# Where the attention stops stand inside the feed-forward slots: five per group, or four that cross the group borders

## The chip, the cores and the metric

One core of a Trainium2 chip runs the whole kernel. The metric is device time in microseconds (us), the median of several executions. PE is the matrix engine, ACT the scalar engine, DVE the vector engine, POOL the general engine (it issues the loads and scales v), and SP the engine that issues the output stores and the transposing DMAs.

## The reference

Retention with a decay per head, then a feed-forward block with a "snake" activation:

```
state = gamma[h]*state + k_t (outer) v_t ;  y_t = (1/sqrt(D)) * q_t @ state      # B=4, H=8, S=768, D=64
x = y laid out as [3072, 512]
h = x @ w_in                      # 512 -> 2048
g = h + sin(alpha*h)^2 / (alpha + 1e-9)
out = g @ w_out                   # 2048 -> 512, float32
```

## The kernel before

**Chunks and groups.** The recurrence is computed in chunks of 128 tokens: 6 chunks for each of 4 batches, 24 in all. They are worked on in the order `P`: P[0..3] are the first chunks of the four batches, then come chunks 1 to 5 of batch 0 (P[4..8]), of batch 1 (P[9..13]), of batch 2 (P[14..18]) and of batch 3 (P[19..23]). Consecutive chunks form groups 0 to 6 of `sizes = [4, 2, 4, 4, 4, 4, 2]` chunks: group 2 is P[6..9], group 3 P[10..13], group 4 P[14..17], group 5 P[18..21], group 6 P[22..23].

**What is done for a chunk j.**

- X(j), `turn`, L205: a transposing DMA on SP's queue writes `qkT` (6 buffers) from the raw `qkr`.
- A(j), `stage_A`: 8 matmuls `pa<-qkT` (L213) on 64-row tiles of PE give the scores, then one DVE multiply with the mask writes `aT` (L217, 2 buffers). `pa` has one buffer.
- M(j), `stage_M`: the mix. 8 matmuls `py<-qkT,s_bd` (L247) with the carried state, 8 matmuls `py<-aT,vr` (L251), and, unless j is the last chunk of its batch, 8 matmuls `ps<-vr,qkr` (L227, `stage_S`) that add to the state; all three are on 128x64 tiles. A DVE multiply writes the chunk's columns of `xT` (L258), and two ACT copies write `s_bd` (L234). `py` has one buffer.
- SK(j): the state of a first chunk, the 8 matmuls of L227 and the two ACT copies, by themselves. It is called ahead of the mix of chunk 1 of a batch.

**The feed-forward of a group.** `phase(g, outs, att, nf)` goes through slots. With `nf=1` there are 16 of them. A slot issues 4 matmuls `ph<-xT,w_in` (L279) of 512 columns, a sine (L282) and a square (L287) on ACT, then whatever stands in `att` for this slot number (a *stop*), then the DVE instruction that writes `gT` (L294), and then a share of `outs`: the matmuls `po<-w_out,gT` (L304) of the group before. A group of 4 tiles gives 64 of these, 4 per slot; group 1, whose two tiles are put out in phase 2, gives 2 per slot. When the 16th matmul of a tile is issued, ACT copies it out (L316) and SP stores it (L317). `ph` and `po` share 4 PSUM buffers, taken in turn.

In phase g the stops hold the attention of group g+1, whose `xT` the first slot of phase g+1 reads. The order on every engine is the order in which the code issues (`manual_schedule`).

Of the kernel before, what the change touches and what calls it, by code (L numbers as in the profile page):

```python
# [15 lines left out]
def kernel(  # L16
# [18 lines left out]
    NCH = S // C  # L35
    NJ = B * NCH
# [4 lines left out]
    FF = d_ff // 128  # L41
# [7 lines left out]
    sizes = [4, 2, 4, 4, 4, 4, 2]  # L49
    assert sum(sizes) == NJ  # L50
    NG = len(sizes)
    groups = [order[sum(sizes[:g]):sum(sizes[:g + 1])] for g in range(NG)]
    place = {j: (g, i) for g, js in enumerate(groups) for i, j in enumerate(js)}
# [148 lines left out]
    def turn(j):  # L202

        st["qkT", j] = work.tile([128, 2 * NP, 128], BF16, name="qkT", tag="qkT", bufs=6)
        nc.sync.dma_start_transpose(out=st["qkT", j], in_=raw["qk", j].rearrange("p i h d -> p (i h d)"))  # L205

    def stage_A(j):
        qkT = st["qkT", j]
        pa = psum.tile([128, 2, NP, 128], F32, name="pa", tag="pa")
        for p in range(NP):  # L210
            for e in range(2):
                r = slice(64 * e, 64 * e + 64)
                nc.tensor.matmul(pa[:, e, p, :], qkT[r, NP + p, :], qkT[r, p, :],  # L213
                                 start=(p == 0), stop=True, skip_group_check=True)
        aT = work.tile([128, 2, NP, 128], BF16, name="aT", tag="aT", bufs=2)
        m = dec.rearrange("p e n t -> p (e n) t") if j % NCH == 0 else mask_bc
        nc.vector.tensor_mul(aT.rearrange("p e n t -> p (e n) t"), pa.rearrange("p e n t -> p (e n) t"), m)  # L217
        st["aT", j] = aT

    def stage_S(j):  # L220
        c = j % NCH
        if c == 0:
            st["ps"] = psum.tile([128, NP, D], F32, name="ps", tag="ps")
        ps = st["ps"]
        for p in range(NP):
            for e in range(2):
                nc.tensor.matmul(ps[64 * e:64 * e + 64, p, :], raw["k", j][:, 2 * p + e, :], raw["v", j][:, 2 * p + e, :],  # L227
                                 start=(c == 0 and p == 0), stop=True, skip_group_check=True)
        return ps

    def keep_S(j, ps):
        for e in range(2):
            r = slice(64 * e, 64 * e + 64)
            nc.scalar.copy(s_bd[(j % NCH + 1) % 2][r, :, r], ps[r, :, :])  # L234

    def stage_M(j):
        c = j % NCH
        g, i = place[j]
        if g not in xT:
            xT[g] = work.tile([128, KS, sizes[g] * C], BF16, name="xT", tag="xT", bufs=3)  # L240
        qkT, aT, vs = st["qkT", j], st["aT", j], raw["v", j]
        py = psum.tile([128, NP, 128], F32, name="py", tag="ty")
        if c > 0:
            for p in range(NP):
                for e in range(2):
                    r = slice(64 * e, 64 * e + 64)
                    nc.tensor.matmul(py[r, p, :], s_bd[c % 2][:, p, r], qkT[:, p, :],  # L247
                                     start=(p == 0), stop=True, skip_group_check=True)
        for p in range(NP):
            for e in range(2):  # L250
                nc.tensor.matmul(py[64 * e:64 * e + 64, p, :], vs[:, 2 * p + e, :], aT[:, e, p, :],  # L251
                                 start=(c == 0 and p == 0), stop=True, skip_group_check=True)
        x = xT[g][:, :, i * C:(i + 1) * C]
        if c == 0:
            nc.scalar.copy(x, py)
            return
        ps = stage_S(j) if c < NCH - 1 else None
        nc.vector.tensor_mul(x, py, qg[:, c])  # L258
        if ps is not None:
            keep_S(j, ps)  # L260
# [40 lines left out]
    def ff_out(g, ts, f):  # L301
        if (g, ts) not in po:
            po[g, ts] = psum.tile([128, d_model], F32, name="po", tag="mm", bufs=4)
        nc.tensor.matmul(po[g, ts], gT[g][:, f, ts * C:(ts + 1) * C], w_out[:, f, :],  # L304
                         start=(f == 0), stop=(f == FF - 1))
        if f == FF - 1:
            take(g, ts)
# [28 lines left out]
    def out_pieces(g, tss):  # L336
        return [lambda ts=ts, f=f: ff_out(g, ts, f) for ts in tss for f in range(FF)]
# [54 lines left out]
    def phase(g, outs, att, nf=1):  # L392

        no, done = len(outs), 0
        for n in range(FF // nf):
            now = Slot(g, n * nf, nf=nf).sq("A")
            for fn in att.get(n, ()):
                fn()
            now.add()
            while done < no * (n + 1) * nf // FF:  # L400
                outs[done]()
                done += 1

    def T(j):
        return lambda: stage_T(j)

    def X(j):
        return lambda: turn(j)

    def A(j):  # L410
        return lambda: stage_A(j)

    def M(j):
        return lambda: stage_M(j)

    def SK(j):
        return lambda: keep_S(j, stage_S(j))
# [3 lines left out]
    P = order  # L421
# [6 lines left out]
    def early(f, tag="mm"):  # L428
        return Slot(0, f, (0, n3), tag=tag)

    a = early(0)
# [6 lines left out]
    a = early(2)  # L438
# [8 lines left out]
    a = early(5)  # L447
# [17 lines left out]
    a = Slot(0, 0, (n3, n4), 4)  # L465
    F((1,), (3,))
    a.sq("A").add()
    a = Slot(0, 8)
    b = Slot(0, 4, (n3, n4), 4)
    a.sq("A").add()  # L470
    a = Slot(0, 9)
# [5 lines left out]
    a = Slot(0, 11)  # L477
# [7 lines left out]
    a = Slot(0, 13)  # L485
# [6 lines left out]
    a = Slot(0, 15)  # L492
# [28 lines left out]
    def fill(n):  # L521
        for _ in range(n):
# [11 lines left out]
    phase(1, outs,  # L534
          {0: [X(P[8])], 1: [A(P[6])], 2: [T(P[7]), X(P[9])], 3: [A(P[7]), M(P[6])], 4: [X(P[10])],
           5: [A(P[8]), M(P[7])], 6: [X(P[11]), A(P[9]), M(P[8]), SK(e1)], 7: [M(P[9])]}, 2)
    for g in range(2, NG):
        att = {}
        if g + 1 < NG:
            js = groups[g + 1]  # L540
            for i, j in enumerate(js):
                a = i * FF // len(js) + 1
                n = P.index(j) + 2
                if n < NJ:
                    att.setdefault(a + 1, []).append(X(P[n]))
                att.setdefault(a, []).append(A(j))
                if i > 0:
                    att[a].append(M(js[i - 1]))
                if j % NCH == 1:
                    att[a].append(SK(j - 1))  # L550
            att.setdefault(FF - 2, []).append(M(js[-1]))
        phase(g, out_pieces(g - 1, range(sizes[g - 1])), att, 1 if sizes[g] > 2 else 2)
    for fn in out_pieces(NG - 1, range(sizes[-1] - 1)):
        fn()
    last_tile(NG - 1, sizes[-1] - 1)
# [28 lines left out]
```

## Time and profile before

| what | value |
|---|---|
| time, median of 5 | 218.57 us (218.03 to 219.02) |
| the profiled execution: time, span | 218.03 us, 216.3 us |
| PE, ACT, DVE busy | 203.8, 162.5, 128.5 us |
| phase 2 (slot 0 to slot 0 of phase 3, start of L279) | 64.86 to 90.72 us |
| phase 3 | 90.72 to 123.21 us |
| phase 4 | 123.21 to 155.45 us |
| phase 5 | 155.45 to 185.31 us |
| PE clock granted | 1.000 |

The span is the time from the first to the last instruction of one profiled execution; its own time lies 1.7 us above its span. The matmul records overlap, since matmuls are pipelined; the distance from one start to the next is what a matmul costs PE. Some matmul records are missing, so a row with x3 may stand for four.

### The profile page before, as it was taken

The page shows a single profiled execution, that of the slowest core. Times are in us where ns is not written, and L with a number is a line of the kernel's source. Part 1 is how long each engine was busy: PE and PEld are TensorE (multiplying, and loading weights), DVE is VectorE, ACT ScalarE, POOL GpSimd, SP SyncE. Part 2 cuts the span into 40 slices and gives each one's busy share as a digit, 9 for nine tenths or more (in the row PEclk, how much of TensorE's full clock was granted, in tenths as well). Part 3 has the DMA queues.
Part 4 walks back from the last instruction along what each step waited for, and adds up shares of the span by engine and source line. Part 5 has one row for each costly group of instructions (what it writes and reads, how often), then busy time and mean ns, then how long its engine had stood idle before and what let it go on. Part 6 is the DMA issues. An engine that isn't in the chain of part 4 may idle for free.

```text
span 216.3 us, 4276 instructions
## 1 busy us (share of the span) xinstructions
PE 203.8 (94%) x1658; PEld 108.9 (50%) x1685; DVE 128.5 (59%) x213; ACT 162.5 (75%) x311; POOL 90.1 (42%) x105
## 2 busy tenths in 40 slices
PE   7898899999889999999999999999999999999994
PEld 3544554466654544445445445455444444555554
DVE  4786669866896767766466556466554455433311
ACT  7688796758879898788778778769768878666630
POOL 8976334998669696696978100000000000000000
PEclk9999999999999999999999999999999999999999
DMA  8999999999999999999999946147111101111112
GB/s 126 148 193 187 206 207 169 154 138 242 143 141 199 141 141 163 127 142 170 134 173 156 69 97 75 25 99 75 28 48 52 48 0 48 52 48 48 52 48 97
DMA packets 100853, 24.93 MB, mean 115 GB/s; under 512 B 93393, under 2 KB 97889, under 8 KB 100833
## 3 DMA queue, kind: packets, MB, share of 16 engines
q0 software_dynamic: 77024, 13.37, 86.3%
q1 hardware_dynamic: 23808, 11.28, 28.8%
q8 instruction: 13, 0.21, 0.4%
q14 instruction: 8, 0.06, 0.1%
HBM read 27.27 MB, written 6.29 MB: 155 GB/s over the span
## 4 chain that ended last, share of the span: by engine, by line
PE 71%; DMA 15%; POOL 4%; DVE 3%; issue 2%; ACT 2%; POOLq 0%; DVEq 0%
PE po L304 32%; PE ph L279 29%; DMA qkr<-in_k_dram 8%; DMA w_in<-in_moe_w_in_dram 4%; DMA qkT<-qkr 3%; PE py L247 3%; PE pa L213 2%; POOL qkr L83 2%; PE py L251 2%; PE poh L327 2%; POOL vr L83 1%; DVE aT L217 1%; PE ps L227 1%; ACT s L282 1%; POOL w_out L94 1%
## 5 line engine op out<-in xcount | busy, mean ns | idle before, releaser
L294 DVE SCALAR_TENSOR_TENSOR gT<-s,rec_alpha,ph 128x512 bf16<-128x512 f32 (+3 forms) x120 | 74.2, 638 | 69.9 <-ACT s L287 69.4
L279 PE MATMUL ph<-xT,w_in 128*128 128x512 bf16 (+3 forms) x478 | 97.9, 336 | 0.7 <-DVE gT L294 0.2
L282 ACT ACTIVATE s<-ph,alpha_sb 128x512 f32<-128x512 f32 (+3 forms) x120 | 69.5, 601 | 34.0 <-PE ph L279 33.9
L304 PE MATMUL po<-w_out,gT 128*128 128x512 bf16 x344 | 90.7, 379 | 3.8 <-issue 2.9
L279 PEld LDWEIGHTS <-w_in 128*128 128x128 bf16 x480 | 45.5, 98 | 42.1 <-issue 1.5
L287 ACT ACTIVATE s<-s 128x512 f32<-128x512 f32 (+1 forms) x94 | 58.4, 621 | 2.6
L304 PEld LDWEIGHTS <-gT 128*128 128x128 bf16 x368 | 33.7, 98 | 36.3 <-issue 0.6
L112 POOL TENSOR_TENSOR vr<-vr,kg 128x512 bf16<-128x512 bf16 x21 | 22.0, 1057 | 19.5 <-DMA vr<-in_v_dram 19.1
L217 DVE TENSOR_TENSOR aT<-pa,mask 128x1024 bf16<-128x1024 f32 x20 | 24.4, 1221 | 0.4 <-PE pa L213 0.4
L83 POOL DMA_DIRECT2D vr<-in_v_dram x24 | 21.8, 909 | 3.8 <-DMA w_in<-in_moe_w_in_dram 1.7
L83 POOL DMA_DIRECT2D qkr<-in_q_dram x23 | 21.3, 926 | 3.7 <-DMA w_out<-in_moe_w_out_dram 1.7
L83 POOL DMA_DIRECT2D qkr<-in_k_dram x23 | 20.6, 894 | 3.8 <-DMA w_out<-in_moe_w_out_dram 3.3
L234 ACT CAST s_bd<-ps 64x256 bf16<-64x256 f32 x40 | 14.4, 359 | 2.6 <-PE ps L227 2.3
L316 ACT COPY o_sb<-po 128x512 f32<-128x512 f32 x23 | 13.1, 575 | 4.0 <-PE po L304 3.9
L258 DVE TENSOR_TENSOR xT<-py,qg 128x512 bf16<-128x512 f32 x20 | 13.7, 684 | 2.3 <-PE py L251 2.1
L213 PE MATMUL pa<-qkT 64*128 64x128 bf16 x192 | 9.5, 219 | 1.5 <-DMA qkT<-qkr 0.9
L345 PE MATMUL spare<-warm 128*128 128x512 bf16 x27 | 9.5, 476 | 1.4 <-DVE warm L131 1.2
L213 PEld LDWEIGHTS <-qkT 64*128 64x128 bf16 x192 | 5.4, 94 | 10.6 <-issue 6.7
L251 PE MATMUL py<-aT,vr 128*64 128x128 bf16 x192 | 9.5, 220 | 0.4 <-DVE aT L217 0.4
L247 PE MATMUL py<-qkT,s_bd 128*64 128x128 bf16 x160 | 8.3, 225 | 0.2 <-DVE xT L258 0.2
L251 PEld LDWEIGHTS <-vr 128*64 128x64 bf16 x192 | 6.8, 110 | 1.3 <-issue 1.0
L247 PEld LDWEIGHTS <-s_bd 128*64 128x64 bf16 x160 | 5.2, 109 | 4.3 <-issue 1.7
(61 smaller groups left out, 75.3 us busy)
## 6 DMA issues: line engine op xcount, KB each, us to landing
out_dram<-o_sb SPq DMA_DIRECT2D x23, 256.0 KB, 2.3
vr<-in_v_dram POOLq DMA_DIRECT2D x24, 128.0 KB, 6.5
qkr<-in_q_dram POOLq DMA_DIRECT2D x23, 128.0 KB, 5.4
qkr<-in_k_dram POOLq DMA_DIRECT2D x23, 128.0 KB, 5.6
w_in<-in_moe_w_in_dram POOLq DMA_DIRECT2D x4, 512.0 KB, 10.7
w_out<-in_moe_w_out_dram POOLq DMA_DIRECT2D x4, 512.0 KB, 14.6
qkT<-qkr SPq DMA_TRANSPOSE x17, 6.4
q<-in_q_dram SPq DMA_DIRECT2D x1, 256.0 KB, 3.2
```

Source lines behind the costliest of these rows:

```text
L83: nc.gpsimd.dma_start(out=t, in_=chunk_of(src, j))
L112: eng.tensor_mul(raw["v", j], raw["v", j], kg[:, j % NCH, :, None].to_broadcast([128, H, D]))
L213: nc.tensor.matmul(pa[:, e, p, :], qkT[r, NP + p, :], qkT[r, p, :], start=(p == 0), stop=True, skip_group_check=True)
L217: nc.vector.tensor_mul(aT.rearrange("p e n t -> p (e n) t"), pa.rearrange("p e n t -> p (e n) t"), m)
L234: nc.scalar.copy(s_bd[(j % NCH + 1) % 2][r, :, r], ps[r, :, :])
L247: nc.tensor.matmul(py[r, p, :], s_bd[c % 2][:, p, r], qkT[:, p, :], start=(p == 0), stop=True, skip_group_check=True)
L251: nc.tensor.matmul(py[64 * e:64 * e + 64, p, :], vs[:, 2 * p + e, :], aT[:, e, p, :], start=(c == 0 and p == 0), stop=True, skip_group_che ...
L279: nc.tensor.matmul(self.ph[:, m, :], w_in[:, i, f * 128:(f + 1) * 128], xT[g][:, i, self.lo:self.hi], start=(m == 0 and i == 0), stop=(i = ...
L282: nc.scalar.activation(out=self.s[:, m, :], in_=self.ph[:, m, :], func=ACTF.Sin, scale=alpha_sb[:, f:f + 1])
L287: nc.scalar.activation(out=self.s, in_=self.s, func=ACTF.Square)
L294: nc.vector.scalar_tensor_tensor(gT[self.g][:, f, self.lo:self.hi], self.s[:, m, :], rec_alpha[:, f:f + 1], self.ph[:, m, :], op0=ALU.mult ...
L304: nc.tensor.matmul(po[g, ts], gT[g][:, f, ts * C:(ts + 1) * C], w_out[:, f, :], start=(f == 0), stop=(f == FF - 1))
```

## The change

Before, the stops of phase g for a group of four are at slots 1, 5, 9, 13 and 14: A of the first chunk alone, three times A of a chunk with M of the chunk ahead of it, and M of the last chunk alone. For the group of two in phase 5 they are at 1, 9 and 14. X stands one slot behind its A.

Afterwards one list of stops runs through phases 2 to 5. Each stop holds A(P[n]), M(P[n-1]), the SK where it is due, and X(P[n+2]), whatever group these chunks belong to. A(P[10]) is by itself in slot 1 of phase 2. The stops are then:

| phase | before | after |
|---|---|---|
| 2 | 1: A10; 5: A11 M10; 9: A12 M11; 13: A13 M12; 14: M13 | 1: A10; 5: A11 M10; 8: A12 M11; 11: A13 M12; 14: A14 M13 SK |
| 3 | 1: A14 SK; 5: A15 M14; 9: A16 M15; 13: A17 M16; 14: M17 | 2: A15 M14; 6: A16 M15; 10: A17 M16; 14: A18 M17 |
| 4 | 1: A18; 5: A19 M18 SK; 9: A20 M19; 13: A21 M20; 14: M21 | 2: A19 M18 SK; 6: A20 M19; 10: A21 M20; 14: A22 M21 |
| 5 | 1: A22; 9: A23 M22; 14: M23 | 6: A23 M22; 14: M23 |

(Numbers are positions in `P`.) On SP, the turns of P[16] to P[23] come one output store earlier than before; those of P[12] to P[15] keep their place among the stores. No instruction is added or removed.

```
+    where = {10: (2, 1)}
+    for g in range(2, NG - 1):
+        first = P.index(groups[g + 1][0])
+        if len(groups[g + 1]) == 2:
+            slots = (6, 14)
+        else:
+            slots = (5, 8, 11, 14) if g == 2 else (2, 6, 10, 14)
+        for i, n in enumerate(slots):
+            where[first + i + 1] = (g, n)
+    atts = {g: {} for g in range(2, NG)}
+    def at(place, fn):
+        atts[place[0]].setdefault(place[1], []).append(fn)
+    for n in range(10, NJ + 1):
+        if n < NJ:
+            at(where[n], A(P[n]))
+        if n > 10:
+            at(where[n], M(P[n - 1]))
+        if n < NJ and P[n] % NCH == 1:
+            at(where[n], SK(P[n] - 1))
+        if n + 2 < NJ:
+            at(where[n], X(P[n + 2]))
     for g in range(2, NG):
-        att = {}
-        if g + 1 < NG:
-            js = groups[g + 1]
-            for i, j in enumerate(js):
-                a = i * FF // len(js) + 1
-                n = P.index(j) + 2
-                if n < NJ:
-                    att.setdefault(a + 1, []).append(X(P[n]))
-                att.setdefault(a, []).append(A(j))
-                if i > 0:
-                    att[a].append(M(js[i - 1]))
-                if j % NCH == 1:
-                    att[a].append(SK(j - 1))
-            att.setdefault(FF - 2, []).append(M(js[-1]))
-        phase(g, out_pieces(g - 1, range(sizes[g - 1])), att, 1 if sizes[g] > 2 else 2)
+        phase(g, out_pieces(g - 1, range(sizes[g - 1])), atts[g], 1 if sizes[g] > 2 else 2)
```

## The prediction

> **What bounds the kernel now.** I read the page's engine shares first, then the PE timeline of phases 2 to 5, then DVE, ACT and SP around the places that change.
>
> ```profile
> PE 203.8 (94%) x1658; PEld 108.9 (50%) x1685; DVE 128.5 (59%) x213; ACT 162.5 (75%) x311; POOL 90.1 (42%) x105
> ```
>
> PE is busy nearly all the time, and from 65 us to the end its timeline shows matmuls end to end. So the question is what a stop costs PE, and where PE waits. The unit is the distance between starts: four 512-column matmuls take 0.865 us, a plain slot with 4 output matmuls 1.727 us (L279 starts at 102.89 and 108.07 are three slots apart), one with 2 output matmuls 1.297 us. The border between phases 2 and 3, and a full stop in phase 4:
>
> ```profile
> 78.43 1.02 PE L279 MATMUL ph<-xT,w_in 128*128 128x512 bf16 x4 [0.18 <-ACT o_sb L316]
> ...
> 87.15 1.03 PE L279 MATMUL ph<-xT,w_in 128*128 128x512 bf16 x4
> 88.41 0.41 PE L247 MATMUL py<-qkT,s_bd 128*64 128x128 bf16 x8 [0.23 <-DVE xT L258]
> 88.64 0.42 PE L251 MATMUL py<-aT,vr 128*64 128x128 bf16 x8
> ...
> 89.42 1.03 PE L279 MATMUL ph<-xT,w_in 128*128 128x512 bf16 x4
> ...
> 92.45 1.03 PE L279 MATMUL ph<-xT,w_in 128*128 128x512 bf16 x4
> 93.41 0.40 PE L213 MATMUL pa<-qkT 64*128 64x128 bf16 x8
> 93.73 0.32 PE L227 MATMUL ps<-vr,qkr 128*64 128x64 bf16 x8
> ...
> 94.86 1.03 PE L279 MATMUL ph<-xT,w_in 128*128 128x512 bf16 x4
> ...
> 132.28 1.03 PE L279 MATMUL ph<-xT,w_in 128*128 128x512 bf16 x4
> 133.24 0.40 PE L213 MATMUL pa<-qkT 64*128 64x128 bf16 x8
> 133.56 0.41 PE L247 MATMUL py<-qkT,s_bd 128*64 128x128 bf16 x8
> 133.81 0.39 PE L251 MATMUL py<-aT,vr 128*64 128x128 bf16 x8
> 134.03 0.29 PE L227 MATMUL ps<-vr,qkr 128*64 128x64 bf16 x8
> ...
> 135.13 1.03 PE L279 MATMUL ph<-xT,w_in 128*128 128x512 bf16 x4
> ```
>
> A stop's price is the distance between the L279 rows around it less one plain slot:
>
> - full (A, M with its state, or A, M and SK; 132.28 to 135.13): 2.85 - 1.73 = 1.12.
> - A alone (124.93 to 127.10, and 157.18 to 159.34): 0.44.
> - A with SK (92.45 to 94.86): 0.68.
> - M with state alone (118.95 to 121.48, and 151.20 to 153.72): 0.80.
> - M without state alone (181.19 to 183.59): 2.40 - 1.73 = 0.67. The same thing at the end of phase 2 costs 89.42 - 87.15 - 1.30 = 0.97: it waits 0.30 for `py`, which the DVE multiply of the chunk ahead, one slot earlier, has not yet read.
>
> The other wait is the first row: slot 9 of phase 2 needs the PSUM buffer of the tile put out at slot 7, while ACT's copy ran from 77.81. Slot 8's L279 started at 76.79 (its L304 at 77.65 less 0.865), so slot 9 was due at 78.08; it came 0.35 late. Check: phase 2 takes 25.86; 16 x 1.297 + 0.44 + 3 x 1.12 + 0.67 = 25.22, so 0.64 is lost, which is 0.35 + 0.30. The same sum for phases 3 to 5 leaves nothing over 0.1.
>
> **What the Trainium skill says.** "TensorEngine Tiling (Array Packing)", section Key Properties: changing the tiling mode drains the TensorE. The trace agrees: 0.96 from an L279 row to the L213 behind it, where four matmuls take 0.865, so 0.10 per change. By this, A alone has two changes, M alone two, A with SK three, a full stop three; joining A and M saves one, joining A with SK and M saves two. The prices agree: 0.44 + 0.80 - 1.12 = 0.12, and 0.68 + 0.67 - 1.12 = 0.23. "PSUM — Partial Sum Buffer", section Engine vs sequencer instructions: VectorE and ScalarE are strict FIFO, and matmuls start in program order. So a late DVE multiply delays everything behind it, and a PE wait stops all of PE; the 88.41 row shows the second.
>
> **The change, part by part.** No work is added; the matmul counts stay.
>
> 1. Joins. M13 with A14 and SK: 0.23 saved, and the 0.30 wait goes, since the multiply that M13 waited for is now three slots back, not one. M17 with A18: 0.12. M21 with A22: 0.80 + 0.43 - 1.12 = 0.11. Sum 0.76, all on PE's path.
> 2. Slots 9 and 13 of phase 2 become 8 and 11. The prices stay; but the stop in slot 8 puts 1.12 of PE work ahead of slot 9's L279, which moves to 76.79 + 1.30 + 1.12 = 79.21. ACT's copy ends at 78.38 (77.81 + 0.57), so it hides, and 0.35 goes. If that cover fails, at most these 0.35 come back.
> 3. ACT in phase 2: sine and square are one per 1.30 us (81.91, 83.20, 84.50, 85.80), just PE's slot. A stop adds 0.73 of ACT copies to 1.12 of PE, so three slots with a stop are 4.63 against 5.01; in the one interval with the tile copy (0.54 between starts) they are 5.17. ACT is then 0.16 late, less than the 0.39 left over in the next. I price it at nothing. DVE: 3 x 0.66 + 1.14 + 0.60 = 3.7 of 5.01. `ph` buffers come back three slots on: slot 11's L279, at about 81.8, needs slot 8's `gT`, which behind mask and `xT` ends at about 81.0. Covered by 0.8.
> 4. The border 2 to 3. In slot 14 DVE must now do the mask of A14 before the `xT` of M13, which the first matmul of phase 3 reads. Slot 13 shows the sequence:
>
> ```profile
> 85.88 0.75 DVE L294 SCALAR_TENSOR_TENSOR gT<-s,rec_alpha,ph 128x512 bf16<-128x512 f32 x1 [0.55 <-ACT s L287]
> 86.54 1.22 DVE L217 TENSOR_TENSOR aT<-pa,mask 128x1024 bf16<-128x1024 f32 x1
> 87.68 0.68 DVE L258 TENSOR_TENSOR xT<-py,qg 128x512 bf16<-128x512 f32 x1
> ```
>
> Its L279 started at 84.73, so `xT` ends 3.63 behind the slot's start; phase 3 begins 2 x 1.30 + 1.12 = 3.71 behind it. The margin is 0.08: I take nothing, and 0 to 0.3 for the range (half a DVE instruction). At borders 3 to 4 and 4 to 5 slots are 0.43 longer, and the margin is 0.9.
> 5. Transposes and SP. A12 comes at 77.8, its turn lands at 75.3 (67.92 + 7.4); A13 at 82.8 against 79.3 (72.85 + 6.4). The tightest is A14:
>
> ```profile
> 78.90 1.43 SPq L205 DMA_TRANSPOSE qkT<-qkr  x1
> 83.40 1.23 SPq L205 DMA_TRANSPOSE qkT<-qkr  x1
> ```
>
> The first is X14, 7.1 to landing, so 86.0; A14's matmuls come at about 87.8 (before: 93.41). X15 lands at 91.5; A15 comes at 94.9. X14 stays behind the same store. X16 and later pass one store, so X16 goes at about 88.5, when its k has landed, in place of 92.83; the store behind it is not due before 91.5, and its issue ties up nobody, as three `o_sb` buffers stand behind it. POOL's order is unchanged, and its v scalings are early: P13 by 76.8 for a mix at 88, the first chunk of batch 2 by 71.1 for SK at 88.6.
>
> Sum: -0.76 - 0.35 = **-1.1 us**. Against the profiled execution (218.03, span 216.3) this gives 216.9 and a span of 215.2. That execution was the fastest of the five shown; taken off the median 218.57 it gives **217.5**. The last phase and the tail only start earlier.
>
> **The rivals.**
>
> - *Joins alone.* The slot 9 wait stays in another place, or the border `xT` is late by 0.3 or more: 0.35 of the gain is left or lost, so about -0.4 to -0.75, or 217.8 to 218.2. For it: the 0.08 margin, and ACT in step with PE with no slack in phase 2. Against: both covers are read off rows of the same sequence. Chance 0.23.
> - *Nothing comes of it.* Denser stops make DVE late in phase 2 by what the joins save; 218.6. For it: the chain sine, square, `gT`, mask, `xT` is 3.63 long in slots of 1.30. Against: the 1.3 us slack of DVE per three slots. Chance 0.07.
> - *Slower.* A14 is pulled forward by 5.6 us, its transpose is not. PE stops for whatever the transpose is late. It lands 1.8 ahead; landings run from 3.1 to 8.8 us. Only from about 10.6 us after issue (3.5 later than X14 took) are both the 1.8 and the gain used up and 0.66 lost, giving 219.2 or more. No turn took that long, but POOL's loads of 128 KB share the DMA engines in this stretch, and the load ahead of it can be late too. Chance 0.07.
>
> **How the numbers follow.** My forecast, -1.3 to -0.9, has the remaining 0.63. A measurement of this kernel can tell some 0.3%, 0.66 us, from no change. Faster than that are the forecast and about half of *joins alone*: 0.75. Within it are the other half and *nothing*: 0.18. Slower: 0.07. The range runs from 217.0 (the forecast's end, with 0.3 for the spread of medians) to 218.4, which takes in *joins alone*.
>
> **What would show it.** In the profile after: phase 2's first L279 to phase 3's takes 25.67 (before 25.86); phase 3 takes 32.11 (32.49), phase 4 32.11 (32.24), phase 5 29.42 (29.86). Every full stop costs 1.12. No wait for `o_sb` at slot 9 and none for `xT` at slot 14. Wrong would be an L279 row at the start of phase 3 that waits for DVE's `xT`, an L213 row at about 88 that waits for the transpose, or a full stop dearer than 1.2.

## The result, and the profile after

The changed kernel takes 217.43 us (median of 22 executions, 216.35 to 217.98) where the kernel before took 218.51 (median of 43, beside them). The ratio is 0.9949, 95% interval 0.9937 to 0.9961: 0.5% or 1.1 us faster. The forecast was 217.5.

The profiled execution of the changed kernel has a span of 215.59 us, only 0.67 under the 216.26 of before. The stretches that the change touches tell more; each runs from the first L279 of its phase to the first of the next:

| stretch, us | before | forecast | after |
|---|---|---|---|
| start of phase 2 | 64.86 | unchanged | 65.28 |
| phase 2 | 25.86 | 25.67 | 25.66 |
| phase 3 | 32.49 | 32.11 | 32.13 |
| phase 4 | 32.24 | 32.11 | 32.13 |
| phase 5 | 29.86 | 29.42 | 29.43 |
| phases 2 to 5 | 120.45 | 119.31 | 119.36 |
| phase 6 to the end | 30.94 | unchanged | 30.96 |

Phases 2 to 5 are 1.09 shorter. The start of phase 2 came 0.42 later in this one execution, and 120.45 - 119.36 - 0.42 - 0.02 leaves 0.65, the difference of the spans (0.67) but for rounding. That start isn't the change's doing: the code ahead of phase 2 is the same in all nine kernels of this study, and in their profiles phase 2 starts anywhere from 64.41 to 66.32. A phase whose code is the same repeats to 0.03, but for one phase in which PE's clock fell (the late turn of P14, below). So a single span can't show this change, and a phase can.

The engine shares of the page after:

```profile
PE 203.2 (94%) x1658; PEld 109.3 (51%) x1685; DVE 127.5 (59%) x213; ACT 162.6 (75%) x311; POOL 90.1 (42%) x105
```

They hardly move. The PE timeline of phase 2 after, slot 8 with its stop up to slot 9, and slot 14 up to the start of phase 3:

```profile
77.19 1.03 PE L279 MATMUL ph<-xT,w_in 128*128 128x512 bf16 x4
78.16 0.40 PE L213 MATMUL pa<-qkT 64*128 64x128 bf16 x8
78.48 0.41 PE L247 MATMUL py<-qkT,s_bd 128*64 128x128 bf16 x8
78.73 0.39 PE L251 MATMUL py<-aT,vr 128*64 128x128 bf16 x8
78.95 0.29 PE L227 MATMUL ps<-vr,qkr 128*64 128x64 bf16 x8
79.17 0.39 PE L304 MATMUL po<-w_out,gT 128*128 128x512 bf16 x1
79.62 1.03 PE L279 MATMUL ph<-xT,w_in 128*128 128x512 bf16 x4
...
87.22 1.03 PE L279 MATMUL ph<-xT,w_in 128*128 128x512 bf16 x4
88.18 0.40 PE L213 MATMUL pa<-qkT 64*128 64x128 bf16 x8
88.51 0.41 PE L247 MATMUL py<-qkT,s_bd 128*64 128x128 bf16 x8
88.75 0.39 PE L251 MATMUL py<-aT,vr 128*64 128x128 bf16 x8
88.98 0.29 PE L227 MATMUL ps<-vr,qkr 128*64 128x64 bf16 x8
89.20 0.39 PE L304 MATMUL po<-w_out,gT 128*128 128x512 bf16 x1
89.64 1.03 PE L279 MATMUL ph<-xT,w_in 128*128 128x512 bf16 x4
90.50 0.59 PE L304 MATMUL po<-w_out,gT 128*128 128x512 bf16 x2
90.94 1.03 PE L279 MATMUL ph<-xT,w_in 128*128 128x512 bf16 x4
```

Slot 8 with its stop takes 79.62 - 77.19 = 2.43: a slot and 1.13. No row has a wait in brackets, neither slot 9's first (it waited for `o_sb` before) nor the mix in slot 14 (it waited for `xT`). Phase 3 starts 90.94 - 89.64 = 1.30 behind slot 15, one plain slot, so it doesn't wait either. DVE in slot 14 shows how near that was:

```profile
89.03 1.22 DVE L217 TENSOR_TENSOR aT<-pa,mask 128x1024 bf16<-128x1024 f32 x1
90.17 0.68 DVE L258 TENSOR_TENSOR xT<-py,qg 128x512 bf16<-128x512 f32 x1
```

`xT` ends at 90.85, 0.09 ahead of its reader. Not all of that was to spare: where PE waits for DVE or ACT in the profiles here, it goes on 0.05 after the end of what it waits for (in the kernel before, at slot 14, `xT` ended at 88.36 and the mix began at 88.41). The change thus had about 0.04 to spare here.

### The profile page after: what moved, and what is told of

Same layout as the page of the kernel before. It is cut to its first block, busy times and chain, and to the rows that moved or that the text cites. A ratio compares the mean times of both kernels' runs of the same rounds, so it can differ in the third digit from the quotient of the medians.

```text
span 215.6 us, 4277 instructions
## 1 busy us (share of the span) xinstructions
PE 203.2 (94%) x1658; PEld 109.3 (51%) x1685; DVE 127.5 (59%) x213; ACT 162.6 (75%) x311; POOL 90.1 (42%) x105
## 4 chain that ended last, share of the span: by engine, by line
PE 74%; DVE 10%; DMA 5%; POOL 4%; ACT 3%; issue 2%; POOLq 0%; DVEq 0%
PE po L304 33%; PE ph L279 31%; DVE gT L294 5%; DMA qkr<-in_k_dram 5%; PE py L247 3%; PE pa L213 2%; POOL qkr L83 2%; DVE aT L217 2%; PE py L251 2%; PE poh L327 2%; ACT s L282 1%; POOL vr L83 1%; ACT s L287 1%; PE ps L227 1%; DVE xT L258 1%
## 5 line engine op out<-in xcount | busy, mean ns | idle before, releaser
L279 PE MATMUL ph<-xT,w_in 128*128 128x512 bf16 (+3 forms) x477 | 97.7, 336 | 1.5 <-DVE gT L294 1.0
L279 PEld LDWEIGHTS <-w_in 128*128 128x128 bf16 x480 | 45.6, 98 | 42.6 <-issue 2.3
L213 PEld LDWEIGHTS <-qkT 64*128 64x128 bf16 x192 | 5.4, 94 | 9.5 <-issue 6.7
L213 PE MATMUL pa<-qkT 64*128 64x128 bf16 x192 | 9.5, 219 | 0.6 <-DVE dec L357 0.2
```

The source lines that it names most:

```text
L279: nc.tensor.matmul(self.ph[:, m, :], w_in[:, i, f * 128:(f + 1) * 128], xT[g][:, i, self.lo:self.hi], start=(m == 0 and i == 0), stop=(i = ...
```

## The experiments

In the order of what they settle. A time is given beside that of the kernel before, executed along with it. The phases decide, since a phase repeats to 0.03 and these times spread by 1 us and more.

**Stops of phase 2 moved, nothing joined.** From the kernel before:

```
-                a = i * FF // len(js) + 1
+                a = (1, 5, 8, 11)[i] if g == 2 else i * FF // len(js) + 1
```

> The kernel before with only the stops of phase 2 moved, to slots 1, 5, 8, 11 and 14; nothing is joined and five stops stay in phases 2 to 4. Theory (two PE waits go by the spacing, the rest by fewer mode changes): both waits of phase 2 go, 0.35 at slot 9 and 0.30 at slot 14, so phase 2 takes 25.2 us in place of 25.86; phases 3, 4 and 5 stay at 32.5, 32.2 and 29.9; the time is 0.65 below the kernel before. Rival (all of the gain comes with the joins, the waits only move): phase 2 takes 25.6 to 25.9 and the time is within 0.3 of before.

Phases 2 to 5 took 25.21, 32.48, 32.24 and 29.86: 0.65 less in all, every bit of it in phase 2. The time was 217.56 against 218.36, ratio 0.9962 (0.9945 to 0.9979), which fits a gain of 0.65 as well as one of 1.1. M13 alone in slot 14, on PE:

```profile
86.44 1.03 PE L279 MATMUL ph<-xT,w_in 128*128 128x512 bf16 x4
87.40 0.41 PE L247 MATMUL py<-qkT,s_bd 128*64 128x128 bf16 x8
87.64 0.39 PE L251 MATMUL py<-aT,vr 128*64 128x128 bf16 x8
...
88.41 1.03 PE L279 MATMUL ph<-xT,w_in 128*128 128x512 bf16 x4
```

The same matmuls as before at slot 14, now 1.97 from L279 to L279 and no wait, where they took 2.27. So more than half of the gain is spacing and needs no join.

**The stop of slot 8 back in slot 9.** From the changed kernel:

```
-            slots = (5, 8, 11, 14) if g == 2 else (2, 6, 10, 14)
+            slots = (5, 9, 11, 14) if g == 2 else (2, 6, 10, 14)
```

> The changed kernel with the second full stop of phase 2 in slot 9 again (slots 5, 9, 11, 14). Theory: slot 9's matmuls again find ACT's copy of the output tile unfinished and wait 0.35, so phase 2 takes 26.0 in place of 25.66; phases 3 to 5 stay at 32.13, 32.13, 29.43; the time is 0.75 below the kernel before. Rival (the wait at slot 9 came from the four-slot spacing as a whole, or is made up further on): phase 2 takes 25.7 and the time is 1.1 below before.

Phase 2 took 26.01, the others 32.13, 32.13 and 29.43. The row is back on PE, and with it ACT's copy, which ends at 79.83, 0.05 before PE goes on:

```profile
78.24 1.03 PE L279 MATMUL ph<-xT,w_in 128*128 128x512 bf16 x4
79.10 0.59 PE L304 MATMUL po<-w_out,gT 128*128 128x512 bf16 x2
79.88 1.02 PE L279 MATMUL ph<-xT,w_in 128*128 128x512 bf16 x4 [0.18 <-ACT o_sb L316]
```

```profile
79.26 0.57 ACT L316 COPY o_sb<-po 128x512 f32<-128x512 f32 x1
```

From slot 8 to slot 9 it is 1.64 in place of 1.30. The time, 217.33 against 218.36, ratio 0.9959 (0.9941 to 0.9977), can't tell 0.75 from 1.1; the phase can.

**Two joins alone.** From the kernel before:

```
-                att.setdefault(a, []).append(A(j))
+                if i > 0 or g < 4:
+                    att.setdefault(a, []).append(A(j))
+                else:
+                    att.setdefault(a, [])
...
+            if g in (3, 4):
+                att.setdefault(FF - 2, []).append(A(groups[g + 2][0]))
             att.setdefault(FF - 2, []).append(M(js[-1]))
```

> The kernel before with two joins only: A18 moves into slot 14 of phase 3 beside M17, A22 into slot 14 of phase 4 beside M21. All other stops stay. Theory (one mode change is saved by a join): phase 3 goes from 32.49 to 32.81 (0.80 becomes 1.12), phase 4 from 32.24 less 0.44 plus 0.33 to 32.13, phase 5 from 29.86 to 29.42; the three together lose 0.23. Rival (the price belongs to the stop's length and not to the number of mode changes): the three together stay at 94.6 within 0.05.

Phases 3 to 5 took 32.81, 32.13 and 29.43, phase 2 its 25.86 of before. The three lose 94.59 - 94.37 = 0.22. (The time of the single execution, 218.84, has a late start of phase 2, 65.88, in it and says nothing here.) A18 joined to M17 in slot 14 of phase 3, on PE:

```profile
119.97 1.03 PE L279 MATMUL ph<-xT,w_in 128*128 128x512 bf16 x4
120.93 0.40 PE L213 MATMUL pa<-qkT 64*128 64x128 bf16 x8
...
122.82 1.03 PE L279 MATMUL ph<-xT,w_in 128*128 128x512 bf16 x4
```

2.85 from L279 to L279, the length of any full stop. With the first experiment the sum closes: 0.65 for two waits, 0.22 for these two joins, and the remaining 1.09 - 0.87 = 0.22 for the join at the border of phases 2 and 3. No run made that join alone, so its share is a remainder. It takes one stop away, as each of the other two does, but two changes of mode where they take one, and it saved twice as much.

**More changes of mode in the same number of stops.** In the changed kernel the scores of P15 to P22 are split around the mix. `half_A` is `stage_A` in two parts: `(0, 1)` issues its first four matmuls, `(2, 3)` the other four and the DVE multiply with the mask. Its definition is left out here:

```
         if n < NJ:
-            at(where[n], A(P[n]))
+            if 15 <= n <= 22:
+                at(where[n], lambda j=P[n]: half_A(j, (0, 1)))
+            else:
+                at(where[n], A(P[n]))
         if n > 10:
             at(where[n], M(P[n - 1]))
+        if 15 <= n <= 22:
+            at(where[n], lambda j=P[n]: half_A(j, (2, 3)))
```

> The changed kernel, but in the eight stops of phases 3 and 4 (P15 to P22) the eight score matmuls are split, four ahead of the mix and four behind it. The number of stops and of matmuls is the same, the number of changes between tile modes in such a stop is four in place of three. Theory (a change of mode costs 0.10 to 0.11): each of the eight stops costs 1.22 in place of 1.12, phases 3 and 4 take 32.5 each in place of 32.13, and the time is 0.8 above the changed kernel, 0.3 below the kernel before. Rival (a stop has a fixed price for leaving and entering the feed-forward matmuls, whatever it holds): phases 3 and 4 stay at 32.13 and the time is 1.1 below before.

Phases 3 and 4 took 32.56 and 32.68, 0.43 and 0.55 more than in the changed kernel. The time was 217.92 against 218.28, ratio 0.9994 (0.9961 to 1.0027): it doesn't exclude the 0.9986 of the theory, nor much else. Two stops of phase 4 on PE, the first that of P19 (L215 are the scores, L263, L267 and L243 the mix and the state, L295 and L320 the feed-forward):

```profile
127.08 1.03 PE L295 MATMUL ph<-xT,w_in 128*128 128x512 bf16 x4
128.04 0.28 PE L215 MATMUL pa<-qkT 64*128 64x128 bf16 x4
128.26 0.41 PE L263 MATMUL py<-qkT,s_bd 128*64 128x128 bf16 x8
128.50 0.39 PE L267 MATMUL py<-aT,vr 128*64 128x128 bf16 x8
128.83 0.29 PE L215 MATMUL pa<-qkT 64*128 64x128 bf16 x4
129.04 0.32 PE L243 MATMUL ps<-vr,qkr 128*64 128x64 bf16 x8
...
130.16 1.03 PE L295 MATMUL ph<-xT,w_in 128*128 128x512 bf16 x4
...
135.34 1.03 PE L295 MATMUL ph<-xT,w_in 128*128 128x512 bf16 x4
136.30 0.29 PE L215 MATMUL pa<-qkT 64*128 64x128 bf16 x4
136.52 0.41 PE L263 MATMUL py<-qkT,s_bd 128*64 128x128 bf16 x8
136.77 0.39 PE L267 MATMUL py<-aT,vr 128*64 128x128 bf16 x8
136.99 0.29 PE L243 MATMUL ps<-vr,qkr 128*64 128x64 bf16 x8
137.21 0.29 PE L215 MATMUL pa<-qkT 64*128 64x128 bf16 x4
...
138.31 1.03 PE L295 MATMUL ph<-xT,w_in 128*128 128x512 bf16 x4
```

Read the tile column: the second stop changes from 128*128 to 64*128, 128*64, 64*128 and back, four changes, and costs 2.97 - 1.73 = 1.24. In P19's stop the SK stands behind the second half of the scores, which I had overlooked in the expectation: five changes, and 3.08 - 1.73 = 1.35. With 1.12 for three changes that is 0.11 to 0.12 for each, with the same number and shapes of matmuls throughout. The two stops shown have five groups of matmuls each and go from one PSUM tile to another equally often; only the order differs, and with it the number of mode changes. So the price goes with the mode and not with the group, and a price of a stop that is fixed, whatever it holds, is excluded. What PE does in these 0.11 us the trace doesn't show.

**The last stop of phase 2 one slot later.** From the changed kernel:

```
-            slots = (5, 8, 11, 14) if g == 2 else (2, 6, 10, 14)
+            slots = (5, 8, 11, 15) if g == 2 else (2, 6, 10, 14)
```

> The changed kernel with the last stop of phase 2 in slot 15 in place of 14. Theory (the chunk's columns of xT are written 3.63 us after the start of their slot, and a slot less leaves 2.42 until phase 3 begins): the first matmul of phase 3 waits 1.2 to 1.3 for DVE, phase 2 takes 26.9 in place of 25.66, and the time is 0.1 to 0.2 above the kernel before. Rival (DVE does the mask and xT earlier when PE is about to wait, so the margin read for slot 14 means little): a wait of under 0.5, phase 2 under 26.2.

Phase 2 took 26.92; the other three stayed. PE at the border, and DVE beside it:

```profile
89.63 0.60 PE L304 MATMUL po<-w_out,gT 128*128 128x512 bf16 x2
91.33 1.02 PE L279 MATMUL ph<-xT,w_in 128*128 128x512 bf16 x4 [1.10 <-DVE xT L258]
```

```profile
89.46 1.22 DVE L217 TENSOR_TENSOR aT<-pa,mask 128x1024 bf16<-128x1024 f32 x1
90.60 0.68 DVE L258 TENSOR_TENSOR xT<-py,qg 128x512 bf16<-128x512 f32 x1
```

Slot 15 began at 87.65, so `xT` ends at 91.28, 3.63 behind it, and PE goes on 0.05 later. The loss of 1.26 is larger than the whole gain of the change, 1.09: slot 14 is the last slot that this border allows. The time of this single execution, 217.77, lies below the forecast, because its phase 2 started at 64.41, the earliest of all.

**The turn of P14 made late.** From the changed kernel:

```
-            at(where[n], X(P[n + 2]))
+            at(where[n], X(P[{14: 15, 15: 14}.get(n + 2, n + 2)]))
```

> The changed kernel with the turns of P14 and P15 issued in the other order, so that P14's comes behind P15's and its wait for P15's keys. Theory (the scores of P14 in slot 14 of phase 2 have some 2 to 3 us in hand for their turn): P14's turn is issued at about 85 us and lands at about 91 to 92, PE waits for it at the L213 row of slot 14 (due at 88) for some 3 us, phase 2 takes about 28.7, and the time is 1.5 to 3 above the kernel before. Rival (the transposes are never on PE's path): phase 2 stays at 25.66 and the time is 1.1 below before.

It was slower: 223.97 (median of 4, 222.09 to 226.30) against 218.28, ratio 1.0239 (1.0188 to 1.0290). The turn went out at 84.73 and landed 6.4 later. PE at slot 14:

```profile
87.25 1.03 PE L279 MATMUL ph<-xT,w_in 128*128 128x512 bf16 x4
91.19 0.40 PE L213 MATMUL pa<-qkT 64*128 64x128 bf16 x8 [2.91 <-DMA qkT<-qkr]
...
92.65 1.80 PE L279 MATMUL ph<-xT,w_in 128*128 128x512 bf16 x4
94.24 1.06 PE L304 MATMUL po<-w_out,gT 128*128 128x512 bf16 x2
95.09 1.57 PE L279 MATMUL ph<-xT,w_in 128*128 128x512 bf16 x4
```

L213 was due at 88.21, so the wait is 2.98, as expected. But phase 2 took 29.79 and phase 3 32.67, 4.67 more than in the changed kernel, so 1.7 are not the wait. They lie between 92.65 and 96.50, where ten feed-forward matmuls take 3.85 and not 2.16. The busy time by stretch, with the granted clock in the third column from the right, says why:

```profile
87.00:91.00 4.00, 1.28 (x6) 0.39 (x4) 1.49 (x2) 2.60 (x5) 2.27 (x4) 1.00 2.11 166
91.00:93.00 2.00, 1.76 (x35) 1.22 (x37) 1.37 (x2) 0.67 (x2) 2.00 (x3) 0.94 1.99 156
93.00:96.00 3.00, 3.00 (x9) 1.08 (x8) 1.24 (x3) 1.55 (x4) 3.00 (x4) 0.50 2.18 169
```

After the stop PE ran at half its clock for a while. The other three executions were longer than the profiled one (222.09), and their mean granted clock was lower, 0.985 against 0.992. An estimate from these means: 0.008 of 220 us is 1.8 us lost to the clock in the profiled execution, about the 1.7 seen, and 0.015 of 222 us is 3.3 in the others, some two such stretches. Where they lay was not profiled.

**The turns of P16 to P23 behind the same stores as before.** From the changed kernel:

```
-            at(where[n], X(P[n + 2]))
+            g, a = where[n]
+            if n >= 14:
+                g, a = (g, a + 2) if a < 14 else (g + 1, 0)
+            at((g, a), X(P[n + 2]))
```

> The changed kernel, but with the turns of P16 to P23 behind the same output store as in the kernel before (each two slots behind its stop, or in slot 0 of the next phase). Theory (the place of these turns on SP's queue costs and brings nothing): phases 2 to 5 take 25.66, 32.13, 32.13 and 29.43 as in the changed kernel. Rival (part of the gain comes from the earlier turns): phases 3 to 5 are longer by 0.1 or more together, at waits for qkT.

25.66, 32.13, 32.13 and 29.43, the changed kernel's phases to the last digit (single execution, 216.85). In phases 2 to 5 the earlier turns neither cost nor bring anything.

No run points to a version ahead of the changed kernel. In its phases 2 to 5 no PE row waits for another engine or a DMA any more; what is left beside the feed-forward is the stops, with their matmuls and the changes of mode that they need. (Nine `po` rows behind a stop carry `[0.16 <-issue]`. Each of them lacks one matmul record, and in phase 2 stops with and without that bracket take the same 2.42 to 2.43 us.)

## Why the prediction was right, point by point

- *What bounds the kernel.* Right. Each edit that took something from PE's path in phases 2 to 5 shortened the phase by that amount, and nothing made it good elsewhere.
- *Joins, 0.76 with the wait in slot 14.* Right. 0.44 for three joins and 0.30 for the wait, 0.74. The size of a mode change, 0.10 to 0.12 by differences of the trace before, came out as 0.11 to 0.12 where it was varied by itself.
- *The wait in slot 9, 0.35.* Right, with its cause: it comes back, 0.35 long, with the stop in slot 9. The trace's bracket gives 0.18 for it, since the bracket counts from the modelled end of the matmul before; the distance of starts gave the 0.35 that came back. The same holds for 0.23 and 0.30 in slot 14.
- *ACT and DVE in phase 2 at nothing.* Right. No PE row of phase 2 waits for them.
- *The border, a margin of 0.08, taken as nothing.* Right, by less than it was put at: 0.09 in the profile after, of which some 0.05 is the time that PE takes to go on after a producer's end, so about 0.04 was left. The sum of the prediction left these 0.05 out, though its rows at 87.68 and 88.41 show them; that the forecast held here is in part luck. A slot later the wait is 1.26.
- *Transposes and SP at nothing.* Right, and easier than read for P14: in this one profile its turn went out at 79.31, landed after 5.9 (7.1 before) at 85.2, and its scores began at 88.18, so 3.0 in hand and not 1.8.
- *The rivals.* "Joins alone" and "nothing comes of it" did not happen: the phases leave no room for them. The place of the slower rival is real: a late turn of P14 does stop PE at slot 14. Its price was too small, since it counted the wait alone; a wait of 2.98 cost 4.67 in the profile. The wait from which it would decide is 1.1 + 0.66 = 1.76 by the prediction's sum; whether the clock falls at such a wait, so that less would be enough, was not tried.

## What to carry to other kernels

On an engine that is full, price an interruption by the distance between the same rows around it less the plain period, and compare kinds of interruption with one another: their differences gave the price of a tile mode change and of two hidden waits without a run. Group small matmuls by tile mode across the borders of a loop, but check for every stop that is moved how long its results have until their reader: here one slot more turned the whole gain into a loss. When a change is worth less than what the start of the kernel varies from execution to execution, measure the stretches that it touches.

## What the hardware showed that was not expected

After PE had stood for 2.98 us at the late turn, its granted clock fell to 0.50 for some 3.4 us (its mean was 0.71 from 92.6 to 93.0, 0.50 from 93.0 to 96.0 and 0.78 from 96.0 to 96.4, and 1.00 after), and the ten matmuls in that stretch took 1.7 us more than usual. The clock did not fall at once: it was still 1.00 in the stop's own matmuls, from 91.2 to 92.6. A wait of 1.26 us in the border experiment was followed by matmuls at the usual distance (91.33, 92.19, 93.05). So the long wait of PE cost half as much again as its own length; where between 1.26 and 2.98 us this sets in was not tried.

That the clock fell because of the wait is likely, but rests on one kernel: all four of its executions had a mean granted clock of 0.985 to 0.992, and the eleven of the kernel before beside them 0.998 or more. In another series 4 of 43 executions of the kernel before had 0.991 to 0.992 as well and took 219.7 to 220.9 us; what set it off there was not profiled.
